# Raw channel-weight blocks fetched ahead of the next k and v, and scaled two rounding steps in front of their use instead of six

## The chip, the cores and the metric

The kernel runs on one core of a Trainium2 chip. The metric is the device time of one execution in microseconds. The profile is a separate execution with the hardware profiler on; its span is 840.7 us.

## The reference

An attention block without softmax is followed by an MLP mixer. Shapes: 8 batches, 8 heads, 576 positions, 64 values a head, so 512 model columns.

```python
kv = np.einsum('bhsd,bhse->bhde', k, v)
out = np.einsum('bhsd,bhde->bhse', q, kv)
rms = np.sqrt(np.mean(out * out, axis=-1, keepdims=True) + 1e-06)
x = out / rms * g_norm                      # then (B,H,S,D) -> (B, S, H*D)

xt = x.transpose(0, 2, 1)
h = np.maximum(xt @ w_tok1, 0.0) @ w_tok2   # w_tok1 576 x 256, w_tok2 256 x 576
u = x + h.transpose(0, 2, 1)
h2 = np.maximum(u @ w_ch1, 0.0) @ w_ch2     # w_ch1 512 x 1536, w_ch2 1536 x 512
return u + h2
```

q, k, v and g_norm are float32. The four weights are float64: the kernel reads each weight as two 32-bit words and rounds it to float32 on the chip.

## The kernel before

**Stages.** The first pass goes over pairs of batches: attention of a pair, then token mixing of that pair, each pair's attention laid beside the token mixing of the pair before. Its result u goes to DRAM. The second pass, channel mixing, reads u back and is the larger part of the time (from about 217 us on). The change lies in the first pass alone.

**Written order.** The work of each engine is issued in the order in which the program names it. `play` walks through lists of step names: `start` (attention of pair 0), `middle` (attention of pair 1, token mixing of pair 0), two `steady` lists, and `last`. One name is one step:

- `kv00`, `kv01`, `kv10`, `kv11`: TensorE products of k and v (side, half of the heads). `e..` copies them from PSUM to `kvp` on ScalarE (L351 on VectorE for pair 0).
- `a..` multiplies q by `kvp` into a `ps_o` bank (two banks), `g..` (L379, VectorE) takes it out with the gain, `q..` (L384, ScalarE) squares it, `t..` (L399) sums the squares, `m`, `r`, `i` make the mean, the root and its inverse (L405, L410, L414 to L419), `s..` (L424, eight ACTIVATEs on ScalarE) or `p..` (L428, GpSimd) scale x by it.
- `h..`, `hr`, `u0` to `u8`: token mixing on TensorE, with relus on ScalarE and the addition of x on VectorE (L118). After `u1`, `u3`, `u5` and `u7` SP stores two blocks of u to DRAM.
- `l00` to `l11`: loads of k and v for the pair after (four DMAs on SP each). `lq0`, `lq1`: the load of q of one batch (one DMA); there are two `qT` buffers. A name with a minus belongs to the attention of the pair before.
- `w2x`, `w3x`, `w4x`: the rounding of token weights. `f0` to `f3`: the fetch of the raw words of channel-weight blocks 0 to 3. A number calls that many rounding steps of the channel weights.

**Rounding.** There are 14 channel-weight blocks, eight of 128 x 768 (0.79 MB of raw words each) and six of 128 x 1024 weights. A block has a fetch into one of four `raw` buffers and seven operations: one scaling on ScalarE (L163), then on VectorE clamp (L166), shift (L170), sign (L174), power (L183), the product with the low words (L187, "lower") and the sum (L118, "both"). `stream` lays the six VectorE operations of all blocks in a row and hangs the others onto them: the scaling of block n + 1 at position -6, that is with the clamp of block n, and the fetch of block n + 4 at position -1, with the sum of block n, since it takes over that block's buffer. Blocks 0 to 3 are fetched by the names `f0` to `f3`. `f1`, `f2` and `f3` take over the buffers of the token-weight blocks whose last readers are `w26`, `w36` and `w46`, and a fetch on SP waits for that. The list of the channel blocks and the stream over them:

```python
channel = ([get_ch1(c, f) for f in range(2) for c in range(NC)]
           + [get_ch2(f) for f in range(NF // 2)])
rounding = stream(channel)
```

SP issues all DMAs of this part but a few at the very start, in the written order.

Of the kernel before, what the change touches and what calls it, by code (L numbers as in the profile page):

```python
# [19 lines left out]
def kernel(  # L20
# [85 lines left out]
    def do(f, *a):  # L106
        return lambda: f(*a)
# [832 lines left out]
    def stream(blocks, ahead=4):  # L940


        steps = [blocks[0][1]]
        for n, block in enumerate(blocks):
            steps += block[2:]
            for at, m, k in ((-6, n + 1, 1), (-1, n + ahead, 0)):
                if m < len(blocks):
                    steps[at] = do(lambda *fs: [f() for f in fs], steps[at], blocks[m][k])
        return iter(steps)
# [40 lines left out]
    for block in tok1[2:] + tok2:  # L990
# [9 lines left out]
        "a00 g00 q00", "a01 g01 q01 t00", "a10 g10 q10 t01 m0 r0", "a11 g11 q11 t10 i0 p00 p01",  # L1000
        "kv10 j6 t11 m1 r1 e10 i1 s10 p11", "kv11 j2 e11", "h00", "a20 g20 q20", "a21 g21 q21 t20",
        "h010 t21 m2 r2", "a30 g30 q30 i2 p20", "a31 g31 q31 t30", "h011 t31 m3 r3 p21", "a40 i3 p30 g40 q40 p31",
        "h012 h013 t40 m4 r4 w21 i4 s40 lq0 l10 l11 lq1"]
    middle = [
        "kv00 e00 l00 w31 w22 w23 w24", "h10 w25 w26 w27 w32 w33 w34", "kv01 e01 l01 w41 w35 w36 w37",
        "h11 w42 w43 w44", "hr w45 w46 w47 f1", "a00 g00 q00 a01 g01 q01 t00 t01", "u0 1", "u1 1",
        "a10 g10 q10 a11 g11 q11 t10 t11 m0 r0", "u2 i0 1 f2", "kv10 e10 s00", "u3 1 s01", "kv11 e11 1",
        "u4 1 f3", "a20 g20 q20 a21 g21 q21 s10", "u5 t20 t21 2", "a40 g40 q40 lq0 l10 l11", "u6 t40 2",
        "a30 g30 q30 a31 g31 q31 lq1 s11", "u7 t30 t31 m2 r2 1 i2 p20 p21 s30", "u8 1 s31"]

    def steady(n0, n1):
# [10 lines left out]
    more = {f"w{n}{k}": f for n, b in enumerate(tok1 + tok2) for k, f in enumerate(b)}  # L1022
    more |= {f"f{n}": b[0] for n, b in enumerate(channel)}
    rounding = stream(channel)

    def keep_warm(n):
# [114 lines left out]
```

## Time and profile before

| | |
|---|---|
| three timed runs | 841.62, 841.60, 842.86 us, median 841.62 |
| span of the profiled execution | 840.7 us |
| TensorE busy, with 6528 matmuls | 814.4 us, 97% of the span |
| VectorE busy | 701.8 us, 83% |
| ScalarE busy | 288.0 us, 34% |
| DMA | 156.57 MB, 186 GB/s on average |
| raw channel blocks f0, f1, f2, f3 issued on SP at | 35.8, 59.7, 61.7, 73.4 us |
| scaling of blocks 0, 1, 2 started on ScalarE at | 56.5, 67.3, 82.3 us |

In the profile, PE is TensorE, DVE is VectorE, ACT is ScalarE, POOL is GpSimd and SP is the engine that issues the transfers. A row of the waits names the engine and line that waited, what it waited for, the total of us, the number of times, and the longest. The chain of waits is followed back from the last instruction: each piece was released by the one above it. TensorE's busy time counts pipelined matmuls and is no measure of its rate; its idle time and its granted clock are the better guide.

### The profile page before, as it was taken

Reading aid. Unit: us, or ns where it says so; the run is one execution under the profiler, and the core shown is the slowest. Engines: PE = TensorE matmul, PEld = TensorE weight load, DVE = VectorE, ACT = ScalarE, POOL = GpSimd, SP = SyncE. Lnnn points to the kernel's source line nnn. Section 1 sums busy time; section 2 is a strip of 40 time slices with the busy share of each in tenths; the row PEclk is TensorE's granted clock in tenths of the full one; section 3 lists DMA queues with packets and bytes.
Section 4 is the critical chain, followed back from the end, with each engine's and each line's share of the span. In section 5 each row is a group of like instructions: output and inputs, shape, how many; then the busy total and the mean of one; then the engine's idle time right before and its main releaser. Section 6 shows DMA issues by size and latency. Waiting matters only on the chain.

```text
span 840.7 us, 16563 instructions
## 1 busy us (share of the span) xinstructions
PE 814.4 (97%) x6528; PEld 720.5 (86%) x6528; DVE 701.8 (83%) x1334; ACT 288.0 (34%) x777; POOL 76.8 (9%) x59
## 2 busy tenths in 40 slices
PE   5996999999999999999999999999999999999997
PEld 5653555554788899999999999999999999999997
DVE  4674989999886888977987997997897797798796
ACT  1344647473111033234323322423423322432321
POOL 1200101010000003003003002000300300300300
PEclk9997999999999999999999999999999999999999
DMA  9994999432435445456446547446545644744642
GB/s 297 323 325 170 342 342 351 150 126 70 179 144 196 166 161 169 136 163 215 140 139 212 168 138 216 164 125 199 192 133 164 200 159 129 232 151 143 199 140 81
DMA packets 67966, 156.57 MB, mean 186 GB/s; under 512 B 5296, under 2 KB 24752, under 8 KB 67888
## 3 DMA queue, kind: packets, MB, share of 16 engines
q1 hardware_dynamic: 66208, 153.77, 56.3%
q10 hardware_dynamic: 1680, 1.74, 0.7%
q8 instruction: 52, 0.85, 0.4%
q14 instruction: 26, 0.21, 0.1%
HBM read 128.35 MB, written 27.13 MB: 185 GB/s over the span
## 4 chain that ended last, share of the span: by engine, by line
PE 83%; DVE 9%; DMA 4%; ACT 1%; issue 1%; SPq 0%; ACTq 0%; DVEq 0%
PE ps_a L127 34%; PE ps_b L127 17%; PE ps_c L127 8%; PE ps_u L127 5%; PE ps_h L127 5%; PE ps_v L127 4%; PE ps_w L127 3%; DMA k_in<-in_k_dram 2%; PE ps_o L127 2%; PE ps_ut L515 2%; PE ps_kv L127 1%; DVE ms L399 1%; DVE sv L118 1%; DMA raw<-in_moe_w_tok_dram 1%; DVE v L118 1%
## 5 line engine op out<-in xcount | busy, mean ns | idle before, releaser
L124 ACT COPY u<-ps_a 128x128 f32<-128x128 f32 (+1 forms) x176 | 60.3, 343 | 176.8 <-PE ps_a L127 162.9
L118 POOL TENSOR_TENSOR v<-v,v 128x768 f32<-128x768 f32 x32 | 58.4, 1854 | 552.6 <-ACT t L124 552.6
L127 PE MATMUL ps_b<-uT,sums 128*128 128x128 f32 x672 | 85.5, 275 | 0.0
L127 PEld LDWEIGHTS ps_b<-uT,sums 128*128 128x128 f32 x672 | 80.2, 192 | 0.0
L127 PE MATMUL ps_a<-uT,w_ch 128*128 128x128 f32 x576 | 78.8, 275 | 0.0
L127 PEld LDWEIGHTS ps_a<-uT,w_ch 128*128 128x128 f32 x576 | 71.5, 192 | 0.1
L118 DVE TENSOR_TENSOR v<-ps_b,u 128x384 f32<-128x384 f32 x112 | 60.2, 549 | 12.9 <-PE ps_b L127 12.9
L127 PE MATMUL ps_u<-h,w_tok 128*128 128x512 f32 (+1 forms) x160 | 68.4, 611 | 0.0
L127 PE MATMUL ps_h<-x,w_tok 128*128 128x512 f32 (+1 forms) x160 | 65.8, 603 | 0.5 <-ACT x L424 0.5
L118 DVE TENSOR_TENSOR v<-v,v 128x768 f32<-128x768 f32 (+1 forms) x70 | 64.1, 925 | 0.3
L118 DVE TENSOR_TENSOR uT<-uT 128x512 f32<-128x512 f32 (+4 forms) x103 | 63.0, 628 | 1.1
L124 ACT COPY t<-ps_a 128x128 f32<-128x128 f32 (+1 forms) x88 | 30.2, 343 | 92.8 <-PE ps_a L127 85.4
L121 ACT ACTIVATE v<-v 128x384 f32<-128x384 f32 (+1 forms) x102 | 49.3, 526 | 30.6 <-DVE v L118 26.6
L127 PE MATMUL ps_a<-uT,w 128*128 128x128 f32 x432 | 58.7, 275 | 0.0
L118 DVE TENSOR_TENSOR u<-ps_a,v 128x384 f32<-128x384 f32 x48 | 26.8, 557 | 32.1 <-PE ps_a L127 31.6
L127 PEld LDWEIGHTS ps_a<-uT,w 128*128 128x128 f32 x432 | 53.4, 192 | 0.0
L127 PEld LDWEIGHTS ps_h<-x,w_tok 128*128 128x128 f32 (+1 forms) x160 | 26.0, 189 | 31.6 <-issue 28.3
L118 DVE TENSOR_TENSOR xg<-xg,r 128x512 f32<-128x512 f32 (+1 forms) x78 | 50.7, 660 | 0.7 <-ACT r L124 0.6
L424 ACT ACTIVATE x<-x,inv 128x64 f32<-128x64 f32 x184 | 45.9, 334 | 10.2 <-DVE inv L419 9.2
L127 PEld LDWEIGHTS ps_u<-h,w_tok 128*128 128x128 f32 (+1 forms) x160 | 25.1, 183 | 27.6 <-issue 22.9
L127 PE MATMUL ps_a<-uT,sums 128*128 128x128 f32 x336 | 46.9, 276 | 1.3 <-ACT t L124 1.3
L127 PE MATMUL ps_a<-sums,sv 128*128 128x128 f32 x336 | 47.3, 277 | 0.9 <-ACT r L124 0.5
(123 smaller groups left out, 1649.9 us busy)
## 6 DMA issues: line engine op xcount, KB each, us to landing
sums<-sums SPq DMA_DIRECT2D x112, 576.0 KB, 3.8
qT<-in_q_dram SPq DMA_DIRECT2D x8, 1152.0 KB, 9.3
xt<-u_dram SPq DMA_DIRECT2D x36, 256.0 KB, 3.5
xg<-u_dram SPq DMA_DIRECT2D x18, 512.0 KB, 5.0
k_in<-in_k_dram SPq DMA_DIRECT2D x16, 512.0 KB, 9.4
u_dram<-x SPq DMA_DIRECT2D x16, 512.0 KB, 3.4
out_dram<-xg SPq DMA_DIRECT2D x16, 512.0 KB, 5.5
sums<-sv SPq DMA_DIRECT2D x14, 576.0 KB, 2.8
```

Source lines behind the costliest of these rows:

```text
L118: keep(engine.tensor_tensor(out=o, in0=a, in1=b, op=op))
L121: keep(nc.scalar.activation(o, a, AF.Relu))
L124: keep(nc.scalar.copy(o, a))
L127: keep(nc.tensor.matmul(*a, **kw))
L399: keep(nc.vector.tensor_reduce(stats_of(c)[0][:, ts(t, H)], sq[c, t], axis=AX.X, op=ALU.add))
L424: keep(nc.scalar.activation(x[:, i], x[:, i], AF.Copy, scale=inv[:, i]))
L515: keep(nc.tensor.transpose(pt[:, c], xt[g, i][:, ts(c, P)], ident))
```

## The change

Two things change. In `stream`, the scaling of a block is issued with the fifth VectorE operation of the block before, two rounding operations ahead of its own clamp, and no longer with the first, six ahead. In the lists `start` and `middle`, the fetches f1, f2 and f3 go forward to the places right behind the last readers of the buffers they take over; the load of q of batch 3 (`lq1`) moves from the end of `start` to the place behind f1, and the load `l00` of pair 2 moves behind that.

```diff
-            for at, m, k in ((-6, n + 1, 1), (-1, n + ahead, 0)):
+            for at, m, k in ((-2, n + 1, 1), (-1, n + ahead, 0)):
                 if m < len(blocks):
                     steps[at] = do(lambda *fs: [f() for f in fs], steps[at], blocks[m][k])
...
-        "h012 h013 t40 m4 r4 w21 i4 s40 lq0 l10 l11 lq1"]
+        "h012 h013 t40 m4 r4 w21 i4 s40 lq0 l10 l11"]
     middle = [
-        "kv00 e00 l00 w31 w22 w23 w24", "h10 w25 w26 w27 w32 w33 w34", "kv01 e01 l01 w41 w35 w36 w37",
-        "h11 w42 w43 w44", "hr w45 w46 w47 f1", "a00 g00 q00 a01 g01 q01 t00 t01", "u0 1", "u1 1",
-        "a10 g10 q10 a11 g11 q11 t10 t11 m0 r0", "u2 i0 1 f2", "kv10 e10 s00", "u3 1 s01", "kv11 e11 1",
-        "u4 1 f3", "a20 g20 q20 a21 g21 q21 s10", "u5 t20 t21 2", "a40 g40 q40 lq0 l10 l11", "u6 t40 2",
+        "kv00 e00 w31 w22 w23 w24", "h10 w25 w26 w27 f1 -lq1 l00 w32 w33 w34", "kv01 e01 l01 w41 w35 w36 w37",
+        "h11 f2 w42 w43 w44", "hr w45 w46 w47 f3", "a00 g00 q00 a01 g01 q01 t00 t01", "u0 1", "u1 1",
+        "a10 g10 q10 a11 g11 q11 t10 t11 m0 r0", "u2 i0 1", "kv10 e10 s00", "u3 1 s01", "kv11 e11 1",
+        "u4 1", "a20 g20 q20 a21 g21 q21 s10", "u5 t20 t21 2", "a40 g40 q40 lq0 l10 l11", "u6 t40 2",
         "a30 g30 q30 a31 g31 q31 lq1 s11", "u7 t30 t31 m2 r2 1 i2 p20 p21 s30", "u8 1 s31"]
```

## The prediction

> **What bounds the kernel now.** I read the page's table of 40 slices first. TensorE is at 9 tenths nearly everywhere, with one dip after the start: the fourth slice (63 to 84 us), where the granted clock dips and the DMA engines idle too.
>
> ```profile
> PE   5996999999999999999999999999999999999997
> ...
> PEclk9997999999999999999999999999999999999999
> DMA  9994999432435445456446547446545644744642
> ```
>
> Second, the waits between 60 and 91 us (engine and line, whom it waited for, us in total, times, longest): TensorE waits for hardly anything but `kvp`, a copy on ScalarE, and ScalarE's one large wait is for a raw weight block.
>
> ```profile
> ACT w_ch L163 <- DMA raw<-in_moe_w_ch_dram: 9.9, 1, 9.9
> ...
> PE ps_o L127 <- ACT kvp L124: 7.8, 2, 4.7
> ...
> PE ps_o L127 <- ACT sq L384: 0.8, 1, 0.8
> ```
>
> Third, the chain of waits from 59 us (start, duration, what), which joins the two:
>
> ```profile
> 49.12 10.51 DMA k_in<-in_k_dram
> ...
> 59.70 7.52 DMA raw<-in_moe_w_ch_dram
> ...
> 67.25 0.02 ACT w_ch L163
> ...
> 68.04 0.59 ACT sq L384
> 68.64 0.02 issue
> 68.66 1.29 DVE ms L399 x2
> ...
> 71.88 3.93 ACT x L424 x16
> 75.81 0.26 ACT kvp L124
> 76.07 0.04 issue
> 76.11 2.93 PE ps_o L127 x12
> 79.04 3.13 PE ps_u L127 x4
> ```
>
> Block 1's raw words (fetch f1) are issued at 59.70, behind the k and v loads l00 and l01, and land at 67.2. Their scaling sits in ScalarE's queue in front of the squares q10 and q11, though the gains they need ended by 60.1. So sums, roots, s00, s01 and the copy e11 are all late, and TensorE, through with u4 at 67.58, stands still from 67.58 to 70.73 and from 71.44 to 76.11. Fourth, three stretches by window (busy us of each engine, clock, DMA share, GB/s): idle, half clock, idle DMA.
>
> ```profile
> 67.50:71.00 3.50, 0.35 (x3) 0.27 (x3) 2.31 (x5) 2.10 (x5) 0.00 (x0) 1.00 0.30 124
> 71.00:76.10 5.10, 0.44 (x4) 0.25 (x3) 4.64 (x10) 4.18 (x17) 0.00 (x0) 0.55 0.45 133
> 76.10:84.00 7.90, 7.89 (x34) 5.08 (x35) 3.19 (x6) 3.90 (x11) 0.00 (x0) 0.64 0.22 89
> ```
>
> From 91 to 147 us TensorE waits for no other engine. From 148 to 177 us the chain runs over VectorE, 97% busy, but TensorE waits only 0.29 us at its end, so both are at their limit together and both move if this hole closes.
>
> **What the Trainium skill says.** "Perfetto Trace Analysis", section "Tensor Engine Instruction (MATMUL, LD_WEIGHTS)", says that ScalarE and VectorE are strict first-in first-out; the squares that sat behind the scaling until 68.04 agree. "TensorE: Matmul & The Clock Gate", section "What's actually happening", says that an idle window of about 3.4 us halves the matmul clock until a busy one restores it; here gaps of 3.15 and 4.67 us go with granted clocks of 0.55 and 0.64. "Perfetto Trace Analysis", section "Roofline", puts one core's DMA ceiling near 435 GB/s; the saturated stretches here move 313 to 402 GB/s over 7 us or more.
>
> **The change part by part.** No instruction is added or removed: 13 scalings on ScalarE move four steps later, and on SP f1, f2, f3 move forward while lq1 (one DMA) and l00 (four) fall behind f1.
>
> *The scaling of block 1* goes from step u1 to step u4 (12 rounding steps lie in this stage before and after). ScalarE then reaches q10 without it. g10 ends at 59.5, g11 at 60.14, so the second square ends at about 60.8 against 69.11: 8.3 us earlier. What follows is the same work (two sums, mean, root, four small VectorE operations, 16 ACTIVATEs of 3.93 us, copy): e11 ends at 76.07 - 8.35 = 67.7. Its other input, kv11, ends at 65.6. TensorE is ready at 67.58 and runs the first four products of a20 (0.45 us at 1.78/16 each) to 68.05, where before it resumed at 76.11: **8.06 us saved**. The clock should not drop: 12 products of ps_o took 2.93 us instead of 12 x 0.111 = 1.33 (1.60 saved), four of ps_u 3.13 instead of the 1.92 of four at 115 us (1.21 saved). Sum 10.87. The next wait, a31 for square q40, was 0.76 us: I follow u5 ending at 71.4, its addition, two sums, the last rounding step, a clamp and g40 (0.69, 1.29, 0.95, 0.55, 0.69) and q40 to 76.1, against 86.75 before: 10.65. I take **10.6**.
>
> *f1 ahead of lq1 and l00.* f1 reuses the buffer read last by w26, whose VectorE operation ended at 45.86; SP is through with l11 at 47.7 and waits, as lq1 does now, for the DMA issued eight before it (38.72 to 48.59). So f1 goes out at 48.7 and lands near 57.5, ten us before it is wanted. lq1 and l00 come about 0.5 us later in issue and 0.79 MB / 0.35 MB per us = 2.2 us later in landing: q lands by 60.5 (57.9 before), wanted by a20 at 67.6; l00 by 63, wanted at 91.3 - 10.6 = 80.7. l01 (wanted at 96.2 - 10.6) shifts likewise. Cost nothing, hidden by these margins. f2 and f3 wait for w36 (50.13) and w46 (53.87), over before SP gets there at about 61; behind them stands the store of u1, which nobody reads until the channel stage. Also nothing.
>
> *The DMA engines.* Through 69 us they are saturated and carry the same bytes plus f3 and u3's store, 1.3 MB or 3.6 us: done at 72.8. f4, the next, is issued after u5 at about 72.5. Backlog against before: 0 to 1 us.
>
> *Scalings 2 to 13.* They now stand two operations, the last product and sum of the block before (0.95 us each, 1.22 for the wide ones), ahead of the clamp that needs them, but ScalarE doesn't wait for those. I replayed its queue at the old times where something long stands in front: scaling 3 behind e01 ends at 102.2 (clamp at 102.34), scaling 7 behind s31 at 142.4 (142.66), scaling 8 at 146.1 (147.30), scaling 12 at 189.3 (190.86). No cost, at narrow margins: from -0.1 to +0.5 us for each of two, thus 0 to 1 us in all. Gain side: scaling 5 waited 6.8 us for its block until 111.6; TensorE did not feel it. Now it stands behind the relus, wanted at 113.9. Between nothing and 0.6 us of gain; I take nothing.
>
> Sum: 840.7 - 10.6 = 830.1 for the profiled execution, 1.26%. The three timed runs are at 841.6 to 842.86; from their median 841.62 I get **831.0 us**.
>
> **The rivals.**
> 1. *DMA becomes the bound (chance 0.12).* From 91 to 140 us its share is 1.05 or more, and the free time in the hole is 0.70 x 3.5 + 0.55 x 5.1 + 0.78 x 7.9 = 11.4 us, hardly more than what I take out. If a backlog of 5 us is carried on, block 5 lands 5 us late against 2.3 us of margin (111.6 to 113.9), and the wait is again in front of squares: 2.7 us back, perhaps twice (scaling 6 waited 1.65): 833.7 to 836.4. Against it: my count of 0 to 1.
> 2. *Only the first hole closes (0.08).* The 16 ACTIVATEs and e11 behind them are ScalarE's own work; if q10's chain meets a VectorE that is still busy, e11 is as far behind TensorE as before: 4.67 stays, 841.6 - 3.15 - 2.8 = 835.7. Against it: VectorE sat idle 8.5 us just there.
> 3. *Slower: clamps wait for scalings (0.05).* If ScalarE regularly reaches a scaling more than lower + both - scaling = 0.95 + 0.95 - 0.93, about 1 us, after VectorE starts the lower product, each clamp waits. Were each to wait for one whole scaling, 7 x 0.93 + 6 x 1.16 = 13.5 us on an engine that is at its limit from 148 us: 841.6 - 10.6 + 13.5 = 844.5. For it: the margins of 0.2 to 0.3 us. Against it: only two of 13 are that narrow.
> 4. *It does not do what it says (0.03):* SP could hold f1 behind another wait, and something else keep q10 back. But with f1 landing at 67.2 as before, the later scaling alone (wanted at 67.7) would not wait: either half suffices. Time then 841.6, about 840 to 843.
>
> **How the numbers follow.** My forecast 0.72: 829.8 to 832.5 (the 0.6 and 1 us of unknown, the 1 us of backlog). Rivals 1 and 2 lie between 833.7 and 836.4, so 829.2 to 836.5 holds some nine in ten before I allow for my own misreading, and eight with it. A measurement here tells about 0.2% (1.7 us) from no change. Faster 0.91 (forecast, rivals 1 and 2, less 0.01), same 0.03, slower 0.06.
>
> **What would show it.** In the profile after: the fourth slice of PE at 9 and its clock at 9; no wait of ScalarE for raw between 55 and 80 us; e11's copy ending near 67.7, a20 unbroken; the raw issue before the third qT near 48.7; the later chain unchanged, 10 to 11 us earlier. Wrong would be a new ScalarE wait for raw near 100, VectorE waits for ScalarE at L166, or TensorE waits for kvp still over 3 us.

## The result and the profile after

| | before | after |
|---|---|---|
| median of four timed runs | 841.61 us (840.94 to 842.86) | 831.94 us (831.58 to 832.03) |
| ratio after / before | | 0.9883, 95% interval 0.9865 to 0.9900 |
| span of the profiled execution | 840.7 us | 830.2 us |
| granted TensorE clock over the span | 0.993 | 0.999 |

The kernel became 1.2% faster: 9.7 us by the medians, 10.5 us by the two profiled spans. The forecast was 831.0 us and 830.1 us for the span.

The slices of the page after, against those shown of before: the fourth of PE and of its clock is full, and the DMA engines are busy through it.

```profile
PE   6999999999999999999999999999999999999997
...
PEclk9999999999999999999999999999999999999999
DMA  9999996422436445365356446546536545644642
```

The same three stretches by window (busy us of each engine, clock, DMA share, GB/s). From 67.5 to 84 us TensorE is busy for 15.7 us where it was busy for 8.7, at full clock.

```profile
67.50:71.00 3.50, 3.48 (x21) 2.47 (x20) 2.77 (x4) 2.44 (x7) 0.00 (x0) 1.00 0.99 386
71.00:76.10 5.10, 4.57 (x30) 2.58 (x28) 4.33 (x7) 2.76 (x10) 0.00 (x0) 1.00 0.66 206
76.10:84.00 7.90, 7.67 (x65) 4.27 (x66) 7.32 (x16) 3.65 (x13) 0.20 (x1) 1.00 1.04 352
```

From 40 to 210 us TensorE waits for one thing only, the squares; the 7.8 us for `kvp` are gone (engine and line, what for, us in total, times, longest):

```profile
PE ps_o L127 <- ACT sq L384: 1.1, 2, 0.8
```

The chain of waits after, from 64.71 us (start, duration, what). It runs over TensorE alone from kv11 through u4 and a20 to u5, with no DMA, scaling or copy in it; the first piece from another engine is the addition of u5.

```profile
64.71 1.32 PE ps_kv L127 x40
66.03 1.91 PE ps_u L127 x4
67.94 0.45 PE ps_o L127 x4
...
68.41 1.60 PE ps_o L127 x12
70.02 1.73 PE ps_u L127 x4
...
71.77 0.69 DVE x L118
```

The timeline of ScalarE after shows why (start, duration, line, operation, number, and in brackets what ended its idle time): s00 and s01 start at 64.18 instead of 71.88, the copy e11 follows at 68.01 instead of 75.71, and the scaling of block 1 comes after it without a wait.

```profile
62.85 0.37 ACT L124 COPY kvp<-ps_kv 128x256 f32<-128x256 f32 x1
64.18 3.93 ACT L424 ACTIVATE x<-x,inv 128x64 f32<-128x64 f32 x16 [0.96 <-DVE inv L419]
68.01 0.35 ACT L124 COPY kvp<-ps_kv 128x256 f32<-128x256 f32 x1
68.26 0.92 ACT L163 ACTIVATE w_ch<-raw 128x768 f32<-128x768 f32 x1
```

### The profile page after: what moved, and what is told of

Read it like the earlier page. It is cut to its first block, busy times and chain, and to the rows that moved or that the text cites. A ratio compares the mean times of both kernels' runs of the same rounds, so it can differ in the third digit from the quotient of the medians.

```text
span 830.2 us, 16562 instructions
## 1 busy us (share of the span) xinstructions
PE 812.6 (98%) x6528; PEld 719.9 (87%) x6528; DVE 701.8 (85%) x1334; ACT 289.1 (35%) x777; POOL 76.9 (9%) x59
## 4 chain that ended last, share of the span: by engine, by line
PE 88%; DVE 9%; issue 1%; DMA 1%; ACT 1%; SPq 0%; ACTq 0%; DVEq 0%
PE ps_a L127 35%; PE ps_b L127 18%; PE ps_c L127 9%; PE ps_h L127 6%; PE ps_u L127 6%; PE ps_v L127 4%; PE ps_w L127 3%; PE ps_o L127 3%; PE ps_ut L515 2%; PE ps_kv L127 2%; DVE sv L118 1%; DMA raw<-in_moe_w_tok_dram 1%; DVE v L118 1%; DVE x L379 1%; DVE ms L399 1%
```

## The experiments

My theory after the result: the hole, the 7.8 us in which TensorE stood still between 67.6 and 76.1 us, came from ScalarE's order. The scaling of block 1 waited for its raw words, and everything written behind it waited too, down to the copy e11. The rivals: the order of the transfers, or the DMA engines' limit, set the time; the squares alone were held up; later scalings hold VectorE's clamps. Each run is compared with the kernel before on the same chip. The ratio has its own estimate and interval and is not the quotient of the two medians beside it; the two differ by up to 0.0008.

| run | us, median | before there | ratio, 95% interval |
|---|---|---|---|
| scalings moved only | 831.67 | 840.54 | 0.9889 (0.9875 to 0.9904) |
| transfers moved only | 831.31 | 840.54 | 0.9885 (0.9871 to 0.9900) |
| f1 in the middle | 836.91 | 840.54 | 0.9951 (0.9934 to 0.9968) |
| scalings one operation later | 836.87 | 840.54 | 0.9952 (0.9935 to 0.9969) |
| hole filled with products | 839.00 | 841.06 | 0.9975 (0.9968 to 0.9982) |
| every scaling twice | 832.68 | 841.06 | 0.9908 (0.9892 to 0.9924) |
| scalings right at the clamp | 831.61 | 841.06 | 0.9894 (0.9878 to 0.9909) |
| g40 first | 831.64 | 841.06 | 0.9893 (0.9877 to 0.9908) |
| 2.1 MB more of transfers | 831.64 | 840.59 | 0.9890 (0.9874 to 0.9907) |
| g40 first, three operations | 830.65 | 840.64 | 0.9885 (0.9868 to 0.9903) |
| changed kernel again | 831.98 | 840.64 | 0.9901 (0.9886 to 0.9916) |

### Each half alone

The scalings alone, on the kernel before:

```diff
-            for at, m, k in ((-6, n + 1, 1), (-1, n + ahead, 0)):
+            for at, m, k in ((-2, n + 1, 1), (-1, n + ahead, 0)):
```

> Only the scalings move (two operations ahead of their clamps); the fetches, lq1 and l00 stay where they were. My theory, that the hole came from ScalarE standing at the scaling of block 1 in front of the squares: f1 still lands near 67.2 us, the scaling is reached near 67.7 to 68.3, so there is no wait, e11 ends near 68 and the whole 10 us are saved: 831 to 833 us. Rival, both halves are needed because block 1 is simply late: the scaling is in front of q20 with no margin, and a wait for raw of 1 to 3 us stays, 834 to 837 us. Rival, the order of the transfers is what counts: no change, 841 to 842 us.

The transfers alone: the lists `start` and `middle` of the change, with the scalings left at -6.

> Only the fetches f1, f2, f3 go forward, and lq1 and l00 behind f1; the scalings stay with the clamp of the block before. My theory: f1 lands near 56.8 us, the scaling of block 1 is reached near 57.7 us and does not wait, q10 starts near 59.9 us as in the changed kernel: 831 to 833 us; the wait of ScalarE for block 5 (6.8 us before) comes back and costs TensorE nothing. Rival, the later scaling is what counts, since an early one holds back squares even without a wait (0.9 us each time, and the 6.8 us): 834 to 838 us.

Measured: 831.67 and 831.31 us, each the whole gain, as the theory had it. With the scalings alone, f1 goes out at 58.79, about where it did, and block 1 is scaled at 67.97 without a wait, right behind the copy e11:

```profile
67.72 0.35 ACT L124 COPY kvp<-ps_kv 128x256 f32<-128x256 f32 x1
67.97 0.91 ACT L163 ACTIVATE w_ch<-raw 128x768 f32<-128x768 f32 x1
```

With the transfers alone it is scaled right behind block 0, near 57 us. The waits of ScalarE from 40 to 200 us in that second run (what waited, for what, us in total, times, longest):

```profile
ACT w_ch L163 <- DMA raw<-in_moe_w_ch_dram: 9.2, 2, 7.2
```

It still waits 9.2 us for later raw blocks, and no time is lost: TensorE's waits for other engines from 48 to 210 us sum to 1.1 us in it, as in the kernel with both halves. A wait of 7.2 us is harmless in one place and one of 9.9 cost 10 us in another.

### Two doses between

f1 alone moved, on the kernel before, to a place between l00 and l01:

```diff
-        "kv00 e00 l00 w31 w22 w23 w24", "h10 w25 w26 w27 w32 w33 w34", "kv01 e01 l01 w41 w35 w36 w37",
-        "h11 w42 w43 w44", "hr w45 w46 w47 f1", "a00 g00 q00 a01 g01 q01 t00 t01", "u0 1", "u1 1",
+        "kv00 e00 l00 w31 w22 w23 w24", "h10 w25 w26 w27 f1 w32 w33 w34", "kv01 e01 l01 w41 w35 w36 w37",
+        "h11 w42 w43 w44", "hr w45 w46 w47", "a00 g00 q00 a01 g01 q01 t00 t01", "u0 1", "u1 1",
```

> A middle dose: the kernel before with f1 alone put between l00 and l01, scalings as before. My theory: f1 is issued near 54.2 us and lands near 62, ScalarE waits some 4 us for it instead of 9.9, the second square of the group ends near 64.1 instead of 69.1, e11 near 71.1 instead of 76.1, TensorE stands still some 3 us in all and its clock may stay up: 833.8 us if it does, up to 836.6 if it drops. Rival, the hole is the DMA engines' (the same bytes before the same use): no gain below 840 us.

Measured 836.91 us, and a profiled execution with a span of 832.6 us. Its waits from 48 to 90 us:

```profile
ACT w_ch L163 <- DMA raw<-in_moe_w_ch_dram: 4.4, 1, 4.4
...
PE ps_o L127 <- ACT kvp L124: 2.6, 1, 2.6
```

A wait of 4.4 us instead of 9.9 leaves a hole of 2.6 us instead of 7.8: 5.5 us less of the wait, 5.2 us less of the hole. That is the chain of the theory. The spread goes with the clock: the profiled execution (834.5 us as timed) kept 0.999 and one of 835.4 us 0.998, three at 0.997 took 836.8 to 837.1 us and one at 0.995 took 839.1. So the hole seems to have dropped the clock in most executions and not in all; only the first of the six was traced.

The scalings moved by one operation only, on the kernel before:

```diff
-            for at, m, k in ((-6, n + 1, 1), (-1, n + ahead, 0)):
+            for at, m, k in ((-5, n + 1, 1), (-1, n + ahead, 0)):
```

> The kernel before with the scaling moved by one operation only (with the shift of the block before instead of the clamp), fetches as before. In ScalarE's written order the scaling of block 1 now stands behind q10, q11 and the root, still ahead of e10, s00, s01 and e11. My theory, that what stands behind the waiting instruction in ScalarE's queue sets the hole: ScalarE waits for raw until 67.2 us (some 4.5 us), e10 ends near 68.4, s00 and s01 follow at once, e11 ends near 72.6 instead of 76.1: 3.5 us saved, 838.2 us, or 835.4 if the clock does not drop. Rival, the squares alone were what held things up: nearly all is saved, 831 to 833 us. Rival, only the landing counts: no change, 841 to 842 us.

Measured 836.87 us. Its chain of waits:

```profile
58.96 7.21 DMA raw<-in_moe_w_ch_dram
...
66.20 0.91 ACT w_ch L163
67.11 0.26 ACT kvp L124
67.38 3.82 ACT x L424 x16
71.19 0.27 ACT kvp L124
...
71.50 2.93 PE ps_o L127 x12
74.43 1.94 PE ps_u L127 x4
```

The squares, sums and root are out of the way now, and yet the copies and the 16 ACTIVATEs still stand behind the scaling. The second part of a20 resumes at 71.50, 4.6 us earlier than before; I had said 3.5, but f1 landed 1 us earlier in this execution. So what is written behind the waiting instruction decides, not the squares alone. The 12 products take 2.93 us, as before the change, and the four of u5 only 1.94 instead of 3.13: behind this one hole of 3.1 us the products are slow for some 3 us, where they were slow for 6 behind the two of before.

### The clock's share

On the kernel before, products of the identity by itself are laid into the hole:

```diff
             for hp in range(HP):
+                if (pair, c, t) == (1, 2, 0) and hp in (0, 2):
+                    keep_warm({0: 13, 2: 20}[hp])
                 matmul(o[:, ts(hp, P)], lhsT=qT[2 * pair + side][:, hp, ts(2 * (c % 2) + t, P)],
```

> The kernel before, with 33 idle products of the identity by itself in TensorE's order (13 ahead of a20, 20 between its second and third pair of heads), about 7.3 us of work laid into the 7.8 us in which TensorE stands still; nothing else moves, the wait for raw stays. It measures the clock's share of the sum by itself. My theory, 2.8 us of the 10.6 come from the dropped clock behind the hole: the clock stays at 1.0 from 71 to 84 us, the 12 products of ps_o take near 1.4 us instead of 2.9, and the time is 838 to 839 us. Rival, the long products behind the hole are waits that the trace draws as products: no change, 840.5 us or more.

Measured 839.00 us, 2.1 us less than before (1.5 to 2.7 by the interval). Its timeline of TensorE:

```profile
70.74 0.61 PE L127 MATMUL ps_o<-kvp,qT 128*128 128x128 f32 x4
71.19 4.63 PE L127 MATMUL ps_j<-ident 128*128 128x128 f32 x40
75.65 1.50 PE L127 MATMUL ps_o<-kvp,qT 128*128 128x128 f32 x12
76.99 1.88 PE L127 MATMUL ps_u<-h,w_tok 128*128 128x512 f32 x4
```

The real products behind the hole are short again, and a31 follows the resumption by 83.47 - 75.65 = 7.8 us instead of 86.75 - 76.11 = 10.6: 2.8 us, the term of the sum. So the long rows were a slow clock and no hidden waits. By the medians the filling saves only 2.1 us. In the execution shown the idle products outlast the hole: f1 went out at 58.97 us instead of 59.70, the copy e11 ended at 75.11, and the last idle product ended near 75.8, so some 0.7 us were lost again. Whether the other executions lost as much is not shown.

### Do late scalings hold VectorE?

On the changed kernel, every scaling of a channel block is issued twice:

```diff
-            keep(nc.scalar.activation(dst, hi.bitcast(F32), AF.Copy, scale=2.0 ** -112))
+            for _ in range(2 if size > S else 1):
+                keep(nc.scalar.activation(dst, hi.bitcast(F32), AF.Copy, scale=2.0 ** -112))
```

> The changed kernel with every scaling of a channel block issued twice (the second writes the same again), so 13.5 us more of ScalarE's work right in front of the clamps. It tests the rival that ended slower. My theory, ScalarE has room almost everywhere: only the clamps of blocks 3 and 7 (margins near 0.2 us) and the copy behind scaling 2 feel it, 832 to 834 us. The rival, VectorE is held by a scaling at most blocks: up to 13 us more, 838 to 845 us.

Then, on the changed kernel, one operation later still:

```diff
-            for at, m, k in ((-2, n + 1, 1), (-1, n + ahead, 0)):
+            for at, m, k in ((-1, n + 1, 1), (-1, n + ahead, 0)):
```

> The changed kernel with each scaling one operation later still, with the sum of the block before, right in front of its clamp in the written order. My theory: in ScalarE's order only the scalings of blocks 1, 2, 6, 7 and 11 move; those of blocks 2 and 7 come behind the copy e00, and the clamp of block 2 waits some 1.5 us on VectorE, which catches up before 137 us: 831.5 to 833 us. Rival, two operations are the least that hides a scaling: each clamp waits near 1 us and the time is 835 us or more.

Measured 832.68 and 831.61 us. VectorE's waits for the scalings, first with every scaling twice (56 to 205 us), where two added lines shift L163 and L166 to L164 and L167:

```profile
DVE w_ch L167 <- ACT w_ch L164: 2.1, 3, 1.4
```

and at the clamp (80 to 205 us):

```profile
DVE w_ch L166 <- ACT w_ch L163: 1.4, 1, 1.4
```

ScalarE is busy for 303.8 us with every scaling twice, instead of 289.1. These 14.7 us cost 0.7 us against the 831.94 us of the changed kernel, which was timed on another chip, and 1.0 us against the other two variants of it on the same chip; TensorE's waits from 48 to 210 us grow by 0.9 us. One operation later costs nothing that can be measured, though block 2's clamp waits the 1.4 us that I had put at 1.5. The slower rival needed a wait at every block; there are three at most. In these runs ScalarE is nearly always ahead of VectorE at the place where a scaling is written.

### Are the DMA engines the limit?

On the changed kernel, two copies of 1.05 MB from DRAM to DRAM, which nobody reads, right behind f3:

```diff
+    ballast = [dram.tile([J * P, DM], F32, name=f"ballast{i}") for i in range(2)]
+    more |= {f"x{i}": do(dma, t, k[i, :LO]) for i, t in enumerate(ballast)}
...
-        "h11 f2 w42 w43 w44", "hr w45 w46 w47 f3", "a00 g00 q00 a01 g01 q01 t00 t01", "u0 1", "u1 1",
+        "h11 f2 w42 w43 w44", "hr w45 w46 w47 f3 x0 x1", "a00 g00 q00 a01 g01 q01 t00 t01", "u0 1", "u1 1",
```

> The changed kernel with two more transfers of 1.05 MB (rows of k copied within DRAM to scratch that nobody reads) issued right behind f3, some 6 us of the DMA engines' time at 350 GB/s. It tests the first rival, a first pass at the DMA engines' limit. My theory: the engines have 1.7 us free before f4, so 4 us or more of backlog are carried on until near 130 us; q of batch 4 (margin 6 us) and k and v (20 us) do not feel it, block 5 comes 3 us or more late for its scaling, and the squares behind it have some 3 us before TensorE wants them: 0 to 3 us lost, 832 to 835 us, with a wait of ScalarE for raw near 103 us. Rival, every us of backlog comes back: 836 us or more.

Measured 831.64 us: nothing lost. The wait of ScalarE that I had expected near 103 us is there:

```profile
ACT w_ch L163 <- DMA raw<-in_moe_w_ch_dram: 1.6, 1, 1.6
```

Fetch f5 goes out at 95.25 instead of 92.31 us, so a backlog of 3 us was carried on, and from 130 to 140 us the DMA share is 0.98 instead of 0.76: there it is worked off. TensorE waits no more than without it. From 48.5 to 130 us the DMA engines of the changed kernel are busy to a share of 0.99 or more, but for 0.66 between 71 and 76 us, and still 3 us of backlog cost nothing. A larger one was not tried.

### What is left of this stretch

On the changed kernel, g40 ahead of two rounding operations:

```diff
-        "u4 1", "a20 g20 q20 a21 g21 q21 s10", "u5 t20 t21 2", "a40 g40 q40 lq0 l10 l11", "u6 t40 2",
+        "u4 1", "a20 g20 q20 a21 g21 q21 s10", "u5 t20 t21", "a40 g40 q40 2 lq0 l10 l11", "u6 t40 2",
```

> The changed kernel with the two rounding operations of step u5 put behind g40 and q40. The 0.76 us in which TensorE waits at a31 for the square q40 should be gone, since g40 no longer stands behind 1.5 us of rounding on VectorE. Theory: 0.7 us less, about 831.2 us, at the edge of what the measurement tells, the row of the wait being the better witness. Rival: fetch f4 goes out 1.3 us later and the k and v behind it too, and the 0.7 us are lost again, 832 us.

Measured 831.64 us, too near to the changed kernel to tell. TensorE's waits from 48 to 210 us:

```profile
PE ps_o L127 <- ACT kvp L124: 0.5, 1, 0.5
PE ps_o L127 <- ACT sq L384: 0.3, 1, 0.3
```

The wait at a31 is gone. Most of it is lost again, though not through late k and v as the rival had it: 0.5 us come back at a00 of the next pair, which waits for a copy e01 that stands behind s30, the scaling of block 2, s31, e00 and s40. Hence one more, with the scalings three operations ahead (-3 in place of -2), so that scaling 2 falls into ScalarE's idle time ahead of s30, beside the changed kernel itself:

> g40 first, as in the run before, and the scalings with the power step of the block before (three operations ahead of the clamp). With g40 first, 0.52 of the 0.76 us came back as a wait of a00 for the copy e01, which stood behind s30, scaling 2, s31, e00 and s40 on ScalarE; at three operations scaling 2 falls into ScalarE's idle time ahead of s30 instead. Theory: both waits are gone, and the time is 0.5 to 0.8 us under the changed kernel on the same chip, 831.0 to 831.3 us if that has 831.8. Rival: scaling 5 now stands ahead of the relus and waits for its block, up to 1 us is lost there, and nothing is gained.

> The changed kernel unaltered, for the comparison on one chip: 831.6 to 832.0 us, TensorE waiting 0.76 us at a31 and nowhere else above 0.3 us between 48 and 200 us.

Measured 830.65 us (830.49 to 830.83) against 831.98 (831.91 to 832.30) for the changed kernel on the same chip. The runs do not overlap, and spans of 828.7 and 830.0 agree, though 0.16% is under what I had called measurable. Both waits are gone; TensorE's waits between 48 and 200 us are, first in this run and then in the changed kernel beside it:

```profile
PE ps_o L127 <- ACT sq L384: 0.3, 1, 0.3
```

```profile
PE ps_o L127 <- ACT sq L384: 1.1, 2, 0.8
```

That is 0.8 us of the 1.3. Another 0.3 us of the profiled span lies ahead of a10 (57.24 against 57.58 us), where the two kernels do not differ; how much of the rest belongs to the edits is not shown. Scaling 5 waits 6.1 us for its block in it, again at no cost.

## Why the prediction was right, point by point

- **The hole's cause and place.** Right, and shown: either half alone removes it, and a shorter wait or a later place shortens it as the chain says. Of the rivals' signs none appears: ScalarE waits for no raw block from 40 to 200 us, both gaps are closed, and no clamp waits for a scaling.
- **When e11 ends.** Said 67.7 us; it ended at 68.36 in an execution whose a10 starts 0.36 us later, so 0.3 us off. The first square did not start at the end of g10, near 59.9, but at 60.32, close to the end of g11, and the two ran back to back; why is not shown. The margin between e11 (67.7) and the end of TensorE's first four products (68.05) absorbed the error: TensorE waits 0.02 us for e11 in the chain.
- **8.06 us of hole.** a20's second part resumes at 68.41 against 76.11; with the 0.36 us of later start, 8.06. That it fits to the hundredth is luck.
- **2.81 us of clock.** Right in sum, in part by luck: the 12 products now take 1.60 us and not 1.33, the four of u5 1.73 and not 1.92, so 1.33 + 1.40 = 2.73 us are saved. Idle products in the hole show 2.8.
- **The median.** It gains 9.7 us and not 10.6. The execution I worked from took 842.49 us, 0.9 above the median of before, and two things in it can account for that. Its clock was 0.993: of the 44 timed executions of before beside the experiments, the 13 at 0.993 took 841.7 us on average and the 27 at 0.995 took 840.6. And its f1 went out 2.2 us after the start of a10 (59.70 and 57.46), where it was 1.1 to 1.3 us in three other runs with the transfers in the old order (scalings moved only, scalings one operation later, hole filled), so that its hole was some 1 us longer than theirs. I had taken this one execution for the typical one. The timed executions were not profiled one by one, so the share of each stays open.
- **a31.** Foretold at 76.1, seen at 76.33, with the same wait of 0.76 us. With the later start that is 10.78 us saved, against 10.65. (The sum puts the end of u5 at 71.4, where its own terms make 71.3.)
- **f1 at 48.7, landing near 57.5.** Issued at 49.09, landed near 56.8. lq1 and l00 behind it held nobody up.
- **No cost of scalings 2 to 13.** Right: no clamp waits for a scaling in the profile after. For block 3 the scaling ends at 91.77 and the clamp starts at 91.93, a margin of 0.16 us.
- **Scaling 5.** Its 6.8 us of waiting are gone, and were worth nothing, as I took it: waits of 6.1 and 7.2 us come back in two of the runs at no cost.
- **Backlog of 0 to 1 us.** f4 goes out at 72.98 (72.5 foretold). My price for a larger one, every us above a margin of 2.3, was too high for the 3 us that were tried, 0.7 us by that sum: the squares behind scaling 5 start at 105.24 instead of 104.10 us, and TensorE's waits do not grow. The 5 us of the first rival were not tried.
- **From 81 us on** all is the old order, shifted: the first product of the channel stage starts at 206.34 instead of 216.77.

## What to carry to other kernels

Look at what is written behind an instruction that waits for a transfer, not at how long it waits: on an engine that works in order, an early step whose transfer lands late blocks the critical copies behind it. Move such a step behind them, or its transfer ahead; if one of the two is enough, the other is only margin. After a hole, count the slow clock that follows as part of its price. And do not take busy DMA engines for the bound before you have seen what a backlog costs.

## What the runs showed of the hardware that I had not expected

A hole of TensorE near 2.6 us seems to lie on an edge: with f1 in the middle the executions fell apart into clocks of 0.999 to 0.995 and times of 834.5 to 839.1 us, while the runs of each kernel with the hole closed or filled lie within 1.2 us of each other. The hole was measured only in the fastest of these executions, where the clock stayed at 1.00 behind it, so the slower ones may have had a longer one. In the run with the scalings moved from -6 to -5, a wait of 3.1 us was followed by a clock of 0.67 between 71 and 76.1 us.
